# Program order on every engine, and state sums in two steps, in a fused retention and feed-forward kernel

## The chip, the cores and the metric

The kernel runs on one core of one Trainium2 chip. The metric is the time of one execution on the device in microseconds (us); lower is better. The kernel before takes 358.58 us, the median of 3 runs (357.47 to 360.11).

Engines are named as the profile names them: PE is TensorE (matrix products), PEld its weight loads, DVE is VectorE, ACT is ScalarE, POOL is GpSimd, SP is the engine that issues most transfers. PEclk is the clock granted to TensorE, as a share of full speed.

## The reference, cut to what matters

The reference is a retention layer (attention with a decaying causal mask and no softmax), then a feed-forward network (FFN) with an ELU between its two products.

```python
# q, k, v: (8 batches, 8 heads, 576 positions, 64), float32
scores = scale * np.matmul(q, k.transpose(0, 1, 3, 2))
Dmat   = np.where(rel >= 0, gamma ** rel, 0.0)         # rel = query - key position, one gamma per head
x      = np.matmul(scores * Dmat, v)                   # then reordered to (4608 tokens, 512)
h      = x @ w_in                                      # 512 -> 2048
g      = np.where(h > 0, h, np.exp(np.minimum(h, 0)) - 1)
out    = g @ w_out                                     # 2048 -> 512
```

Two facts carry the argument. The decay is a power, so it can be moved into factors on `q` and `k`. What earlier positions contribute can then be kept as a running sum of `k^T v`, the state. And nearly all arithmetic lies in the FFN, so the time on TensorE is set there once the FFN is fed.

## The kernel before

**Units.** A batch is cut into five units. Four of them hold 256 positions of four heads, in the order (first half, heads 0 to 3), (first half, heads 4 to 7), (second half, heads 0 to 3), (second half, heads 4 to 7). The fifth, the tail, holds the last 64 positions of all heads. Units are counted through: 0 to 4 are batch 0, 5 to 9 are batch 1. A unit passes through these steps:

- `load`: three transfers from memory (`rqk`, `rv`).
- `cast`: factors on `q` and `k`, written as bf16 (`qkn`), and a cast of `v` (`vn`). Mostly GpSimd.
- `turn_pe` or `turn`: transpose to `qkT`, on TensorE or by a transposing transfer.
- `scores`, `masks`: products inside chunks of 128 positions, and the causal mask.
- `state`, `prefix`: the state after the first chunk (`mid`) and after the second (`end`). VectorE adds, and GpSimd spreads each to a block-diagonal bf16 tile (`s_mid`, `s_end`).
- `inter`, `values`, `put_x`: products with the states and with `v`, then copies into the FFN input `xt`.

TensorE needs `s_mid` for the second chunk of the same unit. The last engine to touch it is GpSimd, which also does most casts of later units.

**Groups.** The FFN works on nine groups of 512 tokens. Group 0 needs units 0 to 3. Group 1 is done in two pieces: 320 columns (tail of batch 0, first half of batch 1: units 4 to 6) and 192 columns (units 7 and 8). Group 2 needs units of batches 1 and 2, and so on.

**Order of instructions.** `pin` marks an instruction as keeping its written place on its engine. TensorE's products, the loads and the transposing transfers are always pinned. All else goes through `soft`, which pins only until a flag falls. From there the framework's scheduler places those instructions, and it may put them ahead of pinned ones that were written earlier.

```python
pin = tc.keep_in_program_order
early = [True]
def soft(ins):
    return pin(ins) if early[0] else ins

def prefix(u, eng=nc.gpsimd):
    ...                                       # st[0], st[1]: the two chunk sums in PSUM
    if T == 0:
        soft(nc.vector.tensor_copy(mid, st[0]))
    else:
        soft(nc.vector.tensor_tensor(mid, st[0], total[w], ALU.add))
    soft(nc.vector.tensor_tensor(end, st[1], mid, ALU.add))
    total[w] = end
    for dst, src in ((s_mid[w], mid), (s_end[w][T], end)):
        soft(eng.tensor_tensor(dst..., src..., diag..., ALU.mult))

def ffn1(g, ft, lo=0, n=TG, relu=False, nf=1):
    ...                                       # four products into ph for each 128 of the 2048 columns
    soft(nc.scalar.activation(e[:, :m], ph[:, :m], AF.Exp))
    if relu:
        soft(nc.scalar.activation(ph[:, :m], ph[:, :m], AF.Relu))
    else:
        soft(nc.vector.tensor_scalar_add(em[:, :m], e[:, :m], -1.0))
    ...                                       # g from ph and e (relu) or em, on VectorE
```

The program has a start (batch 0, nothing else to do on TensorE), a middle (group 0 of the FFN with units 4 to 6 between its pieces), and a rest in which `step()` handles one unit between FFN pieces. `FT` is 4.

```python
for u in range(FT):                           # the start
    scores(u)
    cast_v(u, "s")
    if u + 1 < FT:
        turn_pe(u + 1, "ss")
    new_x()
    if u:
        inter(u - 1)
        values(u - 1)
    state(u)
    warm(2)                                   # filler products
    if u + 1 < FT:
        masks(u)
        prefix(u)
    ...
    if u + 2 < FT:
        cast(u + 2, "v", None)
last_of_start(FT - 1)
...                                           # FFN of group 0; load(FT) stands before the w_out pieces
cast(FT)                                      # the middle
cast(FT + 1, "v", "s")
...
turn_pe(FT)
stretch(FT)
...
cast(FT + 2, "v", "s")                        # unit 6, before the sums of unit 5
...
turn_pe(FT + 1)
stretch(FT + 1)                               # contains prefix(5)
...
turn_pe(FT + 2)
stretch(FT + 2)                               # contains prefix(6)
finish(FT + 2)
early[0] = False                              # from here the order is free
cast(FT + 3)
...
for ft in range(NFT):
    ffn1(1, ft, 0, 320, relu=ft % 2 == 1)     # first piece of group 1
    if ft == 6:
        turn_pe(FT + 3); stretch(FT + 3)
        cast(FT + 4); cast(FT + 5)            # unit 9 is the tail of batch 1
        load(FT + 8)
    ...
def step():
    stretch(u); load(u + 5); cast(u + 3); turn(u + 2)
```

## Time and profile before

The profiled run of the kernel before took 355.82 us (span 354.1 us). A stage is said to start where ScalarE begins the first exponential of its FFN tiles.

| stage | starts at (us) | TensorE busy in it |
|---|---|---|
| group 0 | 27.3 | |
| group 1, 320 columns | 73.3 | |
| group 1, 192 columns | 94.6 | |
| group 2 | 118.9 | |
| groups 3 to 8 | 149.5 | 99% |
| end of span | 354.1 | |

First the page's table of 40 equal slices, kernel before. One slice is 8.85 us. A digit is the busy share in tenths, or the granted clock in tenths.

```profile
PE   3869988187767997899999999999999999999995
...
POOL 5674889914779779234663687287521220100000
PEclk9987999679899998999999999999999999999999
```

From the eighteenth slice on TensorE is at 9. In the first third there are holes (the 1 in the eighth slice, from 62 us) and clock digits of 6 to 8. GpSimd stands at 9 in that slice. The clock digits of the first two slices mean nothing: the clock's record begins at 20.66 us in this trace.

Second, the busy time by stretch, kernel before, from the end of group 0's first outputs. The next three stretches begin with TensorE's first product of a stage, the last one with the stage itself. Columns: the stretch, its length, then for each engine busy us and instructions, then the mean clock, the DMA share, and GB/s.

```profile
core 0: us, PE busy (x) PEld busy (x) DVE busy (x) ACT busy (x) POOL busy (x), PEclk, DMA share, GB/s
49.90:71.60 21.70, 11.30 (x170) 6.45 (x171) 6.72 (x12) 4.73 (x10) 19.62 (x34) 0.85 1.13 266
71.60:92.70 21.10, 15.54 (x189) 9.65 (x186) 14.24 (x32) 12.00 (x31) 8.67 (x16) 0.90 0.73 159
92.70:117.90 25.20, 18.60 (x327) 12.77 (x330) 13.67 (x32) 9.99 (x25) 20.27 (x35) 0.94 1.07 185
117.90:149.50 31.60, 27.70 (x321) 14.33 (x325) 28.34 (x39) 18.71 (x39) 20.23 (x34) 0.95 0.93 199
149.50:335.00 185.50, 183.99 (x1648) 89.78 (x1670) 125.38 (x196) 105.93 (x207) 73.15 (x124) 1.00 0.42 102
```

In the first stretch TensorE works 11.3 of 21.7 us while GpSimd works 19.6. In the last, which is over half of the span, TensorE works 184.0 of 185.5 us at full clock. A change of order can win nothing there.

Third, the timeline of the first stretch, kernel before: start, duration, engine, line, what was written from what. A bracket gives the idle time before an instruction and what ended it.

```profile
60.37 0.28 DVE L363 COPY mid<-x 128x128 f32<-128x128 f32 x1
60.94 0.60 POOL L212 CAST vn<-rv 128x512 bf16<-128x512 f32 x1
61.51 1.17 POOL L199 TENSOR_TENSOR qkt<-rqt,gq 128x256 bf16<-128x256 f32 x2
62.64 0.60 POOL L200 CAST vt<-rvt 64x512 bf16<-64x512 f32 x1
63.21 0.60 POOL L369 TENSOR_TENSOR s_mid_149<-mid,diag 128x256 bf16<-128x256 f32 x1
63.87 0.28 PE L72 MATMUL x<-qkT,s_mid_149 128*128 128x128 bf16 x2 [2.17 <-POOL s_mid_149 L369]
...
65.69 0.28 DVE L363 COPY mid<-x 128x128 f32<-128x128 f32 x1
66.08 1.19 POOL L187 TENSOR_TENSOR qkn<-rqk,gk 128x256 bf16<-128x256 f32 x2
67.20 0.61 POOL L212 CAST vn<-rv 128x512 bf16<-128x512 f32 x1
67.77 1.17 POOL L187 TENSOR_TENSOR qkn<-rqk,gq 128x256 bf16<-128x256 f32 x2
68.92 1.17 POOL L187 TENSOR_TENSOR qkn<-rqk,gk 128x256 bf16<-128x256 f32 x2
70.06 0.60 POOL L369 TENSOR_TENSOR s_mid_150<-mid,diag 128x256 bf16<-128x256 f32 x1
70.71 0.40 PE L72 MATMUL x<-qkT,s_mid_150 128*128 128x128 bf16 x2 [5.87 <-POOL s_mid_150 L369]
```

`mid` of unit 5 was ready at 60.65 us (60.37 + 0.28), but GpSimd first did a `v` cast, then `qkt` and `vt`. Those two are the tail of batch 1, unit 9, which the program writes only beside the seventh tile of group 1. TensorE waited 2.17 us. For unit 6, seven cast instructions (four lines) came between `mid` and `s_mid`, and TensorE waited 5.87 us.

Last, the one instruction that took longest for its kind, from the timeline of group 2, kernel before:

```profile
135.22 6.28 DVE L446 TENSOR_SCALAR em<-e 128x512 bf16<-128x512 f32 x1 [0.36 <-ACT e L442]
```

The same instruction has a median of 0.43 us. Meanwhile GpSimd ran instructions of 0.6 us back to back. This is called a lockout below. The word is a name for an `em` that takes over 1 us beside such a run; that GpSimd is the cause is not shown.

### The profile page before, as it was taken

The page shows a single profiled execution, that of the slowest core. Times are in us where ns is not written, and L with a number is a line of the kernel's source. Part 1 is how long each engine was busy: PE and PEld are TensorE (multiplying, and loading weights), DVE is VectorE, ACT ScalarE, POOL GpSimd, SP SyncE. Part 2 cuts the span into 40 slices and gives each one's busy share as a digit, 9 for nine tenths or more (in the row PEclk, how much of TensorE's full clock was granted, in tenths as well). Part 3 has the DMA queues.
Part 4 walks back from the last instruction along what each step waited for, and adds up shares of the span by engine and source line. Part 5 has one row for each costly group of instructions (what it writes and reads, how often), then busy time and mean ns, then how long its engine had stood idle before and what let it go on. Part 6 is the DMA issues. An engine that isn't in the chain of part 4 may idle for free.

```text
span 354.1 us, 7848 instructions
## 1 busy us (share of the span) xinstructions
PE 310.5 (88%) x3040; PEld 157.0 (44%) x3084; DVE 219.8 (62%) x379; ACT 180.5 (51%) x366; POOL 177.2 (50%) x313
## 2 busy tenths in 40 slices
PE   3869988187767997899999999999999999999995
PEld 1333444045444553344444544544545454444342
DVE  4646845157566699868676876698666665545500
ACT  3446643155343674555555565555656566555611
POOL 5674889914779779234663687287521220100000
PEclk9987999679899998999999999999999999999999
DMA  8959999991899996663469997953320000110021
GB/s 221 325 165 231 387 302 280 234 267 29 219 177 200 253 184 174 179 182 46 101 167 185 210 176 157 236 142 92 79 58 31 31 31 30 49 42 30 31 81 69
DMA packets 100293, 53.86 MB, mean 152 GB/s; under 512 B 44448, under 2 KB 93600, under 8 KB 100256
## 3 DMA queue, kind: packets, MB, share of 16 engines
q1 hardware_dynamic: 97696, 44.97, 56.3%
q0 software_dynamic: 2560, 8.39, 6.9%
q8 instruction: 24, 0.39, 0.5%
q14 instruction: 13, 0.11, 0.1%
HBM read 36.70 MB, written 9.44 MB: 130 GB/s over the span
## 4 chain that ended last, share of the span: by engine, by line
PE 65%; POOL 12%; DMA 9%; issue 5%; DVE 4%; ACT 2%; SPq 2%; POOLq 0%; ACTq 0%; DVEq 0%
PE pm L72 29%; PE ph L72 28%; POOL qkn L187 6%; PE x L72 5%; DMA rqk<-in_k_dram 3%; DVE em L446 3%; PE sc L72 3%; DMA rvt<-in_v_dram 2%; DMA rv<-in_v_dram 2%; DMA wst<-in_moe_w_out_dram 1%; POOL w_in_sb L147 1%; POOL vn L212 1%; SPq L176 1%; POOL s_mid_149 L369 1%; POOL s_mid_150 L369 1%
## 5 line engine op out<-in xcount | busy, mean ns | idle before, releaser
L72 PE MATMUL ph<-xt,w_in_sb 128*128 128x512 bf16 (+2 forms) x612 | 150.9, 369 | 5.3 <-DVE g L453 2.2
L72 PE MATMUL pm<-w_out_sb,g 128*128 128x512 bf16 x564 | 143.6, 380 | 3.4 <-ACT ot L463 2.1
L442 ACT ACTIVATE e<-ph 128x512 f32<-128x512 f32 (+2 forms) x152 | 87.3, 574 | 94.4 <-PE ph L72 82.1
L72 PEld LDWEIGHTS <-w_in_sb 128*128 128x128 bf16 x640 | 60.9, 100 | 68.4 <-issue 11.1
L72 PEld LDWEIGHTS <-g 128*128 128x128 bf16 x576 | 56.0, 98 | 71.7 <-issue 9.1
L451 DVE SCALAR_TENSOR_TENSOR g<-e,ph 128x512 bf16<-128x512 f32 (+2 forms) x80 | 50.2, 632 | 45.0 <-ACT ph L444 44.7
L446 DVE TENSOR_SCALAR em<-e 128x512 bf16<-128x512 f32 (+2 forms) x76 | 53.0, 697 | 36.3 <-ACT e L442 35.8
L466 POOL DMA_DIRECT2D out_dram<-ot x32 | 18.2, 570 | 88.9 <-ACT ot L463 88.9
L453 DVE SCALAR_TENSOR_TENSOR g<-ph,em 128x512 bf16<-128x512 f32 (+2 forms) x80 | 50.6, 637 | 3.5 <-DVE em L446 0.5
L338 ACT CAST xt<-x 128x256 bf16<-128x256 f32 (+1 forms) x71 | 24.2, 417 | 39.9 <-PE x L72 38.3
L444 ACT ACTIVATE ph<-ph 128x512 f32<-128x512 f32 (+2 forms) x76 | 43.3, 570 | 0.0
L285 DVE TENSOR_TENSOR pt<-sc,mask 128x1024 bf16<-128x1024 f32 x31 | 37.7, 1218 | 8.9 <-PE sc L72 8.9
L187 POOL TENSOR_TENSOR qkn<-rqk,gk 128x256 bf16<-128x256 f32 x64 | 39.9, 641 | 3.3 <-DMA rqk<-in_k_dram 3.2
L187 POOL TENSOR_TENSOR qkn<-rqk,gq 128x256 bf16<-128x256 f32 x52 | 31.1, 617 | 14.9 <-PE x L72 13.6
L463 ACT COPY ot<-pm 128x512 f32<-128x512 f32 x36 | 21.1, 589 | 18.4 <-PE pm L72 18.3
L212 POOL CAST vn<-rv 128x512 bf16<-128x512 f32 x26 | 16.3, 626 | 22.8 <-PE x L72 22.8
L72 PE MATMUL sc<-qkT 64*64 64x128 bf16 (+1 forms) x576 | 17.0, 232 | 3.9 <-ACT qkT L235 2.4
L234 PE MATMUL ptr<-ident,qkn 128*128 128x128 bf16 x64 | 9.0, 260 | 7.4 <-POOL diag L135 4.2
L72 PE MATMUL x<-pt,vn 64*64 64x128 bf16 x504 | 14.3, 232 | 1.1 <-DVE pt L381 1.1
L72 PEld LDWEIGHTS <-qkT 64*64 64x64 bf16 x576 | 10.5, 113 | 9.9 <-ACT qkT L235 3.1
L369 POOL TENSOR_TENSOR s_mid_149<-mid,diag 128x256 bf16<-128x256 f32 x16 | 10.0, 622 | 8.4 <-DVE mid L365 6.3
L369 POOL TENSOR_TENSOR s_mid_150<-mid,diag 128x256 bf16<-128x256 f32 x15 | 9.1, 607 | 9.7 <-DVE mid L363 6.5
(77 smaller groups left out, 181.8 us busy)
## 6 DMA issues: line engine op xcount, KB each, us to landing
rqk<-in_q_dram SPq DMA_DIRECT2D x32, 256.0 KB, 5.2
rqk<-in_k_dram SPq DMA_DIRECT2D x32, 256.0 KB, 4.7
rv<-in_v_dram SPq DMA_DIRECT2D x32, 256.0 KB, 5.4
out_dram<-ot POOLq DMA_DIRECT2D x32, 256.0 KB, 3.1
wst<-in_moe_w_in_dram SPq DMA_DIRECT2D x16, 256.0 KB, 5.3
wst<-in_moe_w_out_dram SPq DMA_DIRECT2D x16, 256.0 KB, 4.9
rqt<-in_q_dram SPq DMA_DIRECT2D x8, 128.0 KB, 4.8
rqt<-in_k_dram SPq DMA_DIRECT2D x8, 128.0 KB, 4.0
```

The lines of the kernel that those rows point to most:

```text
L72: pin(nc.tensor.matmul(*a, **kw))
L187: soft(eng.tensor_tensor(natt[u][0][:, i, e], x[:, e], g[:, e], ALU.mult))
L212: soft(engines[eng](natt[u][1], rawt[u][1]))
L285: soft(nc.vector.tensor_tensor(pt.rearrange("p i h n -> p (i h) n"), sc.rearrange("p i (h n) -> p (i h) n", h=2), mask.rearrange("p k e r ...
L338: soft(engines[eng[c]](dst, src[:, :, :, a // 2 : (a + n) // 2]))
L369: soft(eng.tensor_tensor(dst.rearrange("p h (j d) -> p h j d", j=2), src.unsqueeze(2).to_broadcast([P, 2, 2, D]), diag.unsqueeze(1).unsque ...
L442: soft(nc.scalar.activation(e[:, :m], ph[:, :m], AF.Exp))
L444: soft(nc.scalar.activation(ph[:, :m], ph[:, :m], AF.Relu))
L446: soft(nc.vector.tensor_scalar_add(em[:, :m], e[:, :m], -1.0))
L451: soft(nc.vector.scalar_tensor_tensor(dst, e[:, c], -1.0, ph[:, c], ALU.add, ALU.min))
L453: soft(nc.vector.scalar_tensor_tensor(dst, ph[:, c], 0.0, em[:, c], ALU.max, ALU.min))
L463: soft(nc.scalar.copy(ot, pm))
```

## The change

The intent: every engine runs what the program says in the order in which it is written, so that no cast of a later unit stands before a sum that TensorE waits for. For that the casts have to be written where their loads have landed. In the first batch the state sums are split into two steps, `mid` and `end`, with the masks, transposes and copies of the unit placed around them, and the state products move to just after the scores. The arithmetic stays the same, but for four filler products of 512 columns in the last unit of the start. Two casts change their engine: the `v` cast of unit 5 goes from ScalarE to GpSimd, and half of the `k` cast of unit 3 from GpSimd to VectorE.

```diff
-    early = [True]
-    def soft(ins):
-        return pin(ins) if early[0] else ins
 ...                                  # every soft(...) becomes pin(...)
-    def cast_q(u, eng, i=0):
+    def cast_q(u, eng, i=0, es=(0, 1)):
 ...
+    def prefix_mid(u, eng=nc.gpsimd):
+        ...                          # mid, then s_mid
+    def prefix_end(u, parts=(0, 1)):
+        ...                          # part 0: end; part 1: s_end
 ...
     def last_of_start(u):
 ...
             if hl == 0:
-                prefix(u, nc.vector)
-            else:
-                new_x()
+                prefix_mid(u, nc.vector)
             values(u, (hl,), both[hl])
             inter(u, (hl,), both[hl])
             put_x(u, (hl,), both[hl], ("ss", "sv")[hl])
+            warm(2, ...)                                  # fillers
 ...
     for u in range(FT):
         scores(u)
         cast_v(u, "s")
+        new_x()
+        state(u)
         if u + 1 < FT:
+            masks(u)
             turn_pe(u + 1, "ss")
-        new_x()
+        if u == 0:
+            cast(2, "v", None)
+        if u == 1:
+            cast(3, None, None)
+            cast_q(3, nc.vector)
         if u:
             inter(u - 1)
             values(u - 1)
-        state(u)
-        warm(2)
-        if u + 1 < FT:
-            masks(u)
-            prefix(u)
-        if u:
             put_x(u - 1)
             drop(u - 1)
-        if u + 2 < FT:
-            cast(u + 2, "v", None)
+        if u + 1 < FT:
+            prefix_mid(u)
+        if u == 1:
+            cast_q(3, nc.gpsimd, 1, (0,))
+            cast_q(3, nc.vector, 1, (1,))
+        if u + 1 < FT:
+            prefix_end(u)
+        warm(2)
     last_of_start(FT - 1)
+    prefix_end(FT - 1, (0,))
     for i in range(6):
         w_in_piece(i, "p")
+    prefix_end(FT - 1, (1,))
 ...
     for ft in range(8):
-        if ft == 0:
-            load(FT)
         ...                          # w_out pieces, FFN of group 0
-    for u in range(FT + 1, FT + 6):
+    for u in range(FT, FT + 6):
         load(u)
-    cast(FT)
-    cast(FT + 1, "v", "s")
 ...
-    for part in Q[:2]:
-        ffn2(0, 2, part)
+    cast(FT)
+    ffn2(0, 2, Q[0])
+    ffn2(0, 2, Q[1])
+    cast(FT + 1, "v", "p")
+    ffn2(0, 2, Q[2])
+    ffn2(0, 2, Q[3])
     turn_pe(FT)
     stretch(FT)
-    for part in Q[2:]:
-        ffn2(0, 2, part)
-    cast(FT + 2, "v", "s")
     ffn2(0, 3, Q[0])
     ffn2(0, 3, Q[1])
     turn_pe(FT + 1)
     stretch(FT + 1)
+    cast(FT + 2, "v", "s")
 ...
     finish(FT + 2)
-    early[0] = False
     cast(FT + 3)
```

So the change has three parts: the **order** (the flag is gone), the **start** (split sums and what moves around them), and the **middle** (where the load of unit 4 and the casts of units 4 to 6 stand).

More of the change, by code (lines that the diff above doesn't have):

```diff
@@ L146, in w_in_piece @@
         pin(nc.sync.dma_start(t, moe_w_in[j * P : (j + 1) * P, n * 512 : (n + 1) * 512]))
-        soft(engines[eng](w_in_sb[:, j, n * 512 : (n + 1) * 512], t))
+        pin(engines[eng](w_in_sb[:, j, n * 512 : (n + 1) * 512], t))
     def w_out_piece(f, eng):
@@ L151, in w_out_piece @@
         pin(nc.sync.dma_start(t, moe_w_out[f * P : (f + 1) * P, :]))
-        soft(engines[eng](w_out_sb[:, f, :], t))
+        pin(engines[eng](w_out_sb[:, f, :], t))
     rawt, natt, trt, ptt, score_ps, total = {}, {}, {}, {}, {}, {}
@@ L185, in cast_q @@
         g = (gq, gk)[i][:, 2 * T : 2 * T + 2, 4 * w : 4 * w + 4].unsqueeze(3).to_broadcast([P, 2, 4, D])
-        for e in range(2):
-            soft(eng.tensor_tensor(natt[u][0][:, i, e], x[:, e], g[:, e], ALU.mult))
+        for e in es:
+            pin(eng.tensor_tensor(natt[u][0][:, i, e], x[:, e], g[:, e], ALU.mult))
     def cast(u, q="p", v="p"):
@@ L198, in cast @@
             for hs in (slice(0, H // 2), slice(H // 2, H)):
-                soft(nc.gpsimd.tensor_tensor(qkn[:, hs], rqk[:, hs], g[:, hs], ALU.mult))
-            soft(nc.gpsimd.tensor_copy(vn, rv))
+                pin(nc.gpsimd.tensor_tensor(qkn[:, hs], rqk[:, hs], g[:, hs], ALU.mult))
+            pin(nc.gpsimd.tensor_copy(vn, rv))
         else:
@@ L204, in cast @@
             natt[u] = qkn, vn
-            cast_q(u, nc.vector if q == "v" else nc.gpsimd)
-            cast_q(u, nc.gpsimd, 1)
+            if q:
+                cast_q(u, nc.vector if q == "v" else nc.gpsimd)
+                cast_q(u, nc.gpsimd, 1)
             if v:
@@ L211, in cast_v @@
     def cast_v(u, eng):
-        soft(engines[eng](natt[u][1], rawt[u][1]))
+        pin(engines[eng](natt[u][1], rawt[u][1]))
     def turn_tile(u):
@@ L234, in turn_pe @@
                     pin(nc.tensor.transpose(p[:, j], flat(u)[:, lo : lo + P], ident))
-                soft(engines[eng[i]](trt[u][:, i * 4 : i * 4 + 4], p))
+                pin(engines[eng[i]](trt[u][:, i * 4 : i * 4 + 4], p))
     def queries(u, rows, hl, c):
@@ L278, in masks @@
             pt = ppool.tile([ST, 2, HP, ST], BF16, name="ptt", tag="ptt")
-            soft(nc.vector.tensor_tensor(
+            pin(nc.vector.tensor_tensor(
                 pt, sc[:ST, :, : HP * ST].rearrange("p i (h n) -> p i h n", h=HP),
@@ L284, in masks @@
             pt = ppool.tile([P, 2, 2, 2 * P], BF16, name="pt", tag="pt")
-            soft(nc.vector.tensor_tensor(
+            pin(nc.vector.tensor_tensor(
                 pt.rearrange("p i h n -> p (i h) n"), sc.rearrange("p i (h n) -> p (i h) n", h=2),
@@ L326, in put_x @@
             g, off = divmod(b * S + FT * P, TG)
-            soft(nc.scalar.copy(xt_tile(g)[:, :, off : off + ST], xps[0][:, : HP * ST].rearrange("p (h n) -> p h n", h=HP)))
+            pin(nc.scalar.copy(xt_tile(g)[:, :, off : off + ST], xps[0][:, : HP * ST].rearrange("p (h n) -> p h n", h=HP)))
             return
@@ L337, in put_x @@
                 dst = xt_tile(g)[:, 2 * w + h0 : 2 * w + h1, off : off + n].rearrange("p h (r e) -> p h e r", e=2)
-                soft(engines[eng[c]](dst, src[:, :, :, a // 2 : (a + n) // 2]))
+                pin(engines[eng[c]](dst, src[:, :, :, a // 2 : (a + n) // 2]))
                 a += n
@@ L355, in state, with state_ps, block_diag, prefix @@
                         acc_x(c, i, xps[c][i * D : (i + 1) * D, o : o + D], qkn[cs, 1, e, 2 * hl + i], vn[cs, 2 * hl + i, e])
-    def prefix(u, eng=nc.gpsimd):
-        b, T, w, tail = unit(u)
-        st = [x[:, 2 * P : 3 * P].rearrange("p (h d) -> p h d", h=2) for x in xps]
+    mids = {}
+    def state_ps(c):
+        return xps[c][:, 2 * P : 3 * P].rearrange("p (h d) -> p h d", h=2)
+    def block_diag(dst, src, eng):
+        pin(eng.tensor_tensor(
+            dst.rearrange("p h (j d) -> p h j d", j=2), src.unsqueeze(2).to_broadcast([P, 2, 2, D]),
+            diag.unsqueeze(1).unsqueeze(3).to_broadcast([P, 2, 2, D]), ALU.mult,
+        ))
+    def prefix_mid(u, eng=nc.gpsimd):
+        b, T, w, tail = unit(u)
+        mid = rpool.tile([P, 2, D], FP32, name="mid", tag="mid")
+        if T == 0:
+            pin(nc.vector.tensor_copy(mid, state_ps(0)))
+        else:
+            pin(nc.vector.tensor_tensor(mid, state_ps(0), total[w], ALU.add))
+        mids[u] = mid
+        block_diag(s_mid[w], mid, eng)
+    def prefix_end(u, parts=(0, 1)):
+        b, T, w, tail = unit(u)
+        if 0 in parts:
+            total[w] = rpool.tile([P, 2, D], FP32, name="end", tag="end")
+            pin(nc.vector.tensor_tensor(total[w], state_ps(1), mids.pop(u), ALU.add))
+        if 1 in parts:
+            block_diag(s_end[w][T], total[w], nc.gpsimd)
+    def prefix(u):
+        b, T, w, tail = unit(u)
         mid = rpool.tile([P, 2, D], FP32, name="mid", tag="mid")
@@ L362, in prefix @@
         if T == 0:
-            soft(nc.vector.tensor_copy(mid, st[0]))
+            pin(nc.vector.tensor_copy(mid, state_ps(0)))
         else:
-            soft(nc.vector.tensor_tensor(mid, st[0], total[w], ALU.add))
-        soft(nc.vector.tensor_tensor(end, st[1], mid, ALU.add))
+            pin(nc.vector.tensor_tensor(mid, state_ps(0), total[w], ALU.add))
+        pin(nc.vector.tensor_tensor(end, state_ps(1), mid, ALU.add))
         total[w] = end
-        for dst, src in ((s_mid[w], mid), (s_end[w][T], end)):
-            soft(eng.tensor_tensor(
-                dst.rearrange("p h (j d) -> p h j d", j=2), src.unsqueeze(2).to_broadcast([P, 2, 2, D]),
-                diag.unsqueeze(1).unsqueeze(3).to_broadcast([P, 2, 2, D]), ALU.mult,
-            ))
+        block_diag(s_mid[w], mid, nc.gpsimd)
+        block_diag(s_end[w][T], end, nc.gpsimd)
     def last_of_start(u):
@@ L378, in last_of_start @@
         ptt[u] = pt
-        both = [[ps_h.tile([P, 512], FP32, name="o2", tag="ph") for _ in range(2)], None]
+        both = [[ps_h.tile([P, 512], FP32, name="o2", tag="ph") for _ in range(2)],
+                [ps_m.tile([P, 512], FP32, name="o3", tag="pm"), ps_h.tile([P, 512], FP32, name="o3", tag="ph")]]
         for hl in range(2):
-            soft(nc.vector.tensor_tensor(
+            pin(nc.vector.tensor_tensor(
                 pt[:, :, hl], sc.rearrange("p i (h n) -> p i h n", h=2)[:, :, hl],
@@ L391, in last_of_start @@
             put_x(u, (hl,), both[hl], ("ss", "sv")[hl])
+            warm(2, both[1][1] if hl == 0 else ps_s.tile([P, 2, 512], FP32, name="warm", tag="sc")[:, 0])
         drop(u)
@@ L441, in ffn1 @@
         m = n * nf
-        soft(nc.scalar.activation(e[:, :m], ph[:, :m], AF.Exp))
+        pin(nc.scalar.activation(e[:, :m], ph[:, :m], AF.Exp))
         if relu:
-            soft(nc.scalar.activation(ph[:, :m], ph[:, :m], AF.Relu))
+            pin(nc.scalar.activation(ph[:, :m], ph[:, :m], AF.Relu))
         else:
-            soft(nc.vector.tensor_scalar_add(em[:, :m], e[:, :m], -1.0))
+            pin(nc.vector.tensor_scalar_add(em[:, :m], e[:, :m], -1.0))
         for f in range(nf):
@@ L450, in ffn1 @@
             if relu:
-                soft(nc.vector.scalar_tensor_tensor(dst, e[:, c], -1.0, ph[:, c], ALU.add, ALU.min))
+                pin(nc.vector.scalar_tensor_tensor(dst, e[:, c], -1.0, ph[:, c], ALU.add, ALU.min))
             else:
-                soft(nc.vector.scalar_tensor_tensor(dst, ph[:, c], 0.0, em[:, c], ALU.max, ALU.min))
+                pin(nc.vector.scalar_tensor_tensor(dst, ph[:, c], 0.0, em[:, c], ALU.max, ALU.min))
     def ffn2(g, it, fts, pool=None, tag="pm"):
@@ L462, in ffn2, with warm @@
             ot = opool.tile([P, DM], FP32, name="ot", tag="ot")
-            soft(nc.scalar.copy(ot, pm))
+            pin(nc.scalar.copy(ot, pm))
             i0 = g * TG + it * P
             store = nc.sync if g == NTG - 1 else nc.gpsimd
-            soft(store.dma_start(out[i0 : i0 + P, :], ot))
-    def warm(n):
-        if n:
-            d = ps_h.tile([P, TG], FP32, name="warm", tag="ph")
-            for _ in range(n):
-                mm(d, ident, zero, start=True, stop=True)
+            pin(store.dma_start(out[i0 : i0 + P, :], ot))
+    def warm(n, d=None):
+        d = ps_h.tile([P, TG], FP32, name="warm", tag="ph") if d is None else d
+        for _ in range(n):
+            mm(d, ident, zero, start=True, stop=True)
     def last_unit(g):
```

## The prediction

> **What bounds the kernel now.** There are two regimes. In the busy-time table by stretch, TensorE is busy 187.6 of 189.2 us from 145.8 to 335 us at a granted clock of 1.00: nothing but TensorE work matters there. The first 145.8 us are different. TensorE is busy 12.0 of 22.6 us (49.9 to 72.5), 14.8 of 20.2 (72.5 to 92.7), 18.6 of 25.2 (92.7 to 117.9) and 24.1 of 27.9 (117.9 to 145.8), and the clock is 0.50 from 25.3 to 30.9 us. There the chain of waits runs through GpSimd casts and loads. From 50 to 120 us it gives GpSimd `qkn` 24%.
>
> **What costs the time.** In the timeline, casts of later units stand ahead of the state sums on GpSimd. `mid` was written at 60.4 us and its `s_mid` only began at 63.2; TensorE sat idle 2.17 us. The next one cost 5.87 us (`mid` 65.7, `s_mid` 70.1), and the clock then stayed halved until about 76 us. Similar waits of 0.9 to 2.1 us follow at 92, 102, 106, 111 and 115 us. At 135.2 us a VectorE `em`, 0.43 us at its median, took 6.28 us beside an unbroken GpSimd run. [...]
>
> **What the change moves.** No arithmetic to speak of is added: about four more filler matmuls (0.22 us each at full clock).
> 1. Start. The split sums and earlier state matmuls take the k-cast to transpose to sum loop (4.54 us per unit now) apart. Following my estimate in the new order with traced durations, FFN work starts near 23.8 us instead of 25.3, and fillers probably keep the clock up (now 5.6 us at 0.50 lose 2.8 us). The weight casts begin earlier, so the load queue's gap at 18.8 to 22.5 us (19 to 45 GB/s) closes. Gain about 4 us by 50 us.
> 2. 50 to 72.5 us. In program order `s_mid` follows `mid` at once: both waits shrink to the 1.5 to 2 us of mask, copy and product. Casting unit 6 (the third of the second batch) after the sums costs about 2 us back. Second-group FFN starts near 64 us; cumulative gain 8 us.
> 3. 72.5 to 120 us. GpSimd loses its hoisted lead, but its idle time (8.3 us before 80.7, 4.2 before 88.4, 4.1 before 98.8) shrinks. This stretch stays bound by GpSimd, about 4.2 us per unit (five casts of 0.6, two sums of 0.6). Cumulative gain 10 to 13 us.
> 4. After that TensorE bounds; no gain. The 6.28 us lockout may go, or come back elsewhere, as GpSimd runs become longer.
>
> Shrinking the sum somewhat for lockouts and cold clocks, I expect 346 us, range 338 to 353: faster by over 2% 0.80, within 2% 0.17, slower 0.03.
>
> **What would show each step.** First `ph` matmul near 24 us with 0.22 us per 512 columns, not 0.43; waits of TensorE on `s_mid` under 2 us around 55 to 65 us; first 320-column `ph` matmul near 64 us; GpSimd near full from there to 105 us; 99% busy TensorE afterwards, its stretch unshortened.
>
> **What would make it wrong.** A TensorE still at half clock in the start [...]; `em` starved beside the longer GpSimd runs, directly on the path while 320-column FFN tiles take 0.65 us each; transposing loads waiting for late casts between 85 and 95 us; in-order queues adding waits in the steady part, where free order was already at 99%.

The sum came to 10 to 13 us. That fillers keep the clock up is the author's expectation. The clock of that trace was at half from 65.0 to 75.3 us, a little less long than stated. One slip in it: unit 6 is the third of units 4, 5 and 6, but the second unit of the second batch. Unit 4 is the tail of the first.

## The result, and the profile after

| | median (us) | runs | range |
|---|---|---|---|
| before | 359.28 | 4 | 357.47 to 360.11 |
| after | 339.89 | 4 | 339.27 to 341.77 |

The ratio is 0.9476, with a 95% interval of 0.942 to 0.9531: faster. A ratio in this document is the mean time of one kernel's fast runs over that of the other's fast runs of the same rounds, so it is not quite the ratio of the medians that are quoted. The prediction's class was right, and its range of 338 to 353 us holds the result. Its centre of 346 us was 6 us too high.

The profiled run of the changed kernel took 339.58 us, a typical one, while that of before was a fast one. The two traces differ by 16.2 us in span, the medians by 19.4 us. The traces therefore explain 16.2 us.

| stage | before starts at | after starts at | gain so far (us) |
|---|---|---|---|
| group 0 | 27.3 | 23.2 | 4.1 |
| group 1, 320 columns | 73.3 | 65.3 | 8.0 |
| group 1, 192 columns | 94.6 | 84.1 | 10.5 |
| group 2 | 118.9 | 108.3 | 10.6 |
| groups 3 to 8 | 149.5 | 133.8 | 15.8 |
| last exponential | 334.6 | 318.3 | 16.2 |
| end of span | 354.1 | 337.9 | 16.2 |

The page's slices, kernel after (8.45 us each):

```profile
PE   3877997777769999999999999999999999999995
...
POOL 5586955528989799243585568566665120000100
PEclk9999999599899999999999999999999999999999
```

The hole of 1 in TensorE's row is gone. One clock digit of 5 is left, at about 60 us.

The busy time by stretch, kernel after; columns and stages as before:

```profile
46.10:63.60 17.50, 12.24 (x170) 6.86 (x171) 7.41 (x14) 4.82 (x10) 9.97 (x17) 0.88 1.12 292
63.60:82.60 19.00, 15.04 (x189) 9.50 (x186) 13.84 (x31) 11.91 (x31) 9.79 (x17) 0.93 0.30 77
82.60:107.30 24.70, 18.65 (x327) 13.07 (x330) 14.86 (x34) 10.06 (x26) 23.74 (x42) 0.93 1.11 233
107.30:133.80 26.50, 26.14 (x321) 13.58 (x325) 23.01 (x39) 18.76 (x40) 23.03 (x39) 1.00 1.26 222
133.80:318.70 184.90, 183.57 (x1648) 89.73 (x1670) 119.14 (x196) 105.81 (x207) 81.03 (x135) 1.00 0.49 117
```

The first stretch shrinks from 21.7 to 17.5 us, and GpSimd's work in it from 34 instructions to 17: the casts of later units have left it. They come back in the third stretch (35 instructions before, 42 after) and in the last (124 and 135). The fourth stretch, group 2, shrinks by 5.1 us: TensorE is now busy 99% of it at full clock. The last is the same within 0.6 us.

The timeline of the two sums, kernel after:

```profile
55.73 0.28 DVE L387 COPY mid<-x 128x128 f32<-128x128 f32 x1
56.16 0.60 POOL L359 TENSOR_TENSOR s_mid_149<-mid,diag 128x256 bf16<-128x256 f32 x1 [4.17 <-DVE mid L387]
...
61.70 0.28 DVE L387 COPY mid<-x 128x128 f32<-128x128 f32 x1
62.07 0.60 POOL L359 TENSOR_TENSOR s_mid_150<-mid,diag 128x256 bf16<-128x256 f32 x1 [2.69 <-DVE mid L387]
...
62.73 0.40 PE L67 MATMUL x<-qkT,s_mid_150 128*128 128x128 bf16 x2 [1.58 <-POOL s_mid_150 L359]
```

Now GpSimd waits for `mid` (4.17 and 2.69 us idle) and starts the sum at once. The product with `s_mid` of unit 5 has no wait listed, that of unit 6 has 1.58 us in place of 5.87.

The longest waits of TensorE between 48 and 146 us (what waited, what for; us in total, times, longest). First before, then after:

```profile
PE x L72 <- POOL s_mid_150 L369: 10.5, 4, 5.9
PE x L72 <- POOL s_mid_149 L369: 6.8, 4, 2.2
```

```profile
PE x L67 <- POOL s_mid_150 L359: 2.7, 2, 1.6
PE sc L67 <- DMA qkT<-qkn: 2.5, 2, 2.0
...
PE x L67 <- POOL s_mid_149 L359: 0.8, 1, 0.8
```

Waits for `s_mid` fall from 17.3 to 3.5 us. A wait for transposing transfers (`qkT<-qkn`) is new.

### The profile page after: what moved, and what is told of

Same layout as the page of the kernel before. It is cut to its first block, busy times and chain, and to the rows that moved or that the text cites. A ratio compares the mean times of both kernels' runs of the same rounds, so it can differ in the third digit from the quotient of the medians.

```text
span 337.9 us, 7844 instructions
## 1 busy us (share of the span) xinstructions
PE 305.2 (90%) x3044; PEld 156.5 (46%) x3088; DVE 207.5 (61%) x379; ACT 179.3 (53%) x365; POOL 179.3 (53%) x314
## 4 chain that ended last, share of the span: by engine, by line
PE 73%; DVE 9%; DMA 6%; POOL 4%; ACT 4%; issue 2%; SPq 1%; DVEq 0%; ACTq 0%; POOLq 0%
PE pm L67 34%; PE ph L67 30%; PE x L67 4%; PE sc L67 3%; DVE pt L281 2%; DMA wst<-in_moe_w_in_dram 2%; DMA rqk<-in_q_dram 2%; DVE g L472 2%; DMA qkT<-qkt 1%; DVE em L467 1%; DMA qkT<-qkn 1%; DVE g L474 1%; POOL qkn L182 1%; SPq L171 1%; ACT xt L334 1%
## 5 line engine op out<-in xcount | busy, mean ns | idle before, releaser
L67 PE MATMUL ph<-xt,w_in_sb 128*128 128x512 bf16 (+2 forms) x611 | 147.3, 361 | 4.6 <-DVE g L474 1.3
L67 PEld LDWEIGHTS <-w_in_sb 128*128 128x128 bf16 x640 | 60.0, 99 | 65.6 <-issue 6.8
L467 DVE TENSOR_SCALAR em<-e 128x512 bf16<-128x512 f32 (+2 forms) x76 | 42.1, 554 | 32.2 <-ACT e L463 32.1
L182 POOL TENSOR_TENSOR qkn<-rqk,gk 128x256 bf16<-128x256 f32 x63 | 37.9, 621 | 4.2 <-DMA rqk<-in_k_dram 4.2
L359 POOL TENSOR_TENSOR s_mid_150<-mid,diag 128x256 bf16<-128x256 f32 x15 | 9.2, 615 | 26.1 <-DVE mid L387 12.6
L208 POOL CAST vn<-rv 128x512 bf16<-128x512 f32 x27 | 17.9, 663 | 0.0
L67 PEld LDWEIGHTS <-qkT 64*64 64x64 bf16 x576 | 10.5, 112 | 13.3 <-ACT qkT L231 5.1
L230 PE MATMUL ptr<-ident,qkn 128*128 128x128 bf16 x64 | 8.0, 252 | 7.4 <-DVE qkn L182 5.2
L67 PE MATMUL x<-pt,vn 64*64 64x128 bf16 x496 | 13.6, 226 | 0.0
```

The source lines that it names most:

```text
L67: pin(nc.tensor.matmul(*a, **kw))
L182: pin(eng.tensor_tensor(natt[u][0][:, i, e], x[:, e], g[:, e], ALU.mult))
L359: pin(eng.tensor_tensor(dst.rearrange("p h (j d) -> p h j d", j=2), src.unsqueeze(2).to_broadcast([P, 2, 2, D]), diag.unsqueeze(1).unsquee ...
L467: pin(nc.vector.tensor_scalar_add(em[:, :m], e[:, :m], -1.0))
```

## The experiments

**The theory and its rivals.** Theory A (order): the free order lets casts of later units in ahead of the sums; most of the gain is the order alone, and the start alone is worth 4 us at most. Rival B (placement): the new start and middle bring the gain themselves, whatever the order. Rival C (lockout): the main gain is that the long `em` (2.7 to 6.3 us in the kernel before) are gone. Twelve kernels were run, each beside runs of the kernel before. Medians are compared within a call; across calls, ratios.

### The order alone: p_only

```diff
 # from before
     finish(FT + 2)
-    early[0] = False
     cast(FT + 3)
```

> The kernel before with one line taken out, so that VectorE, ScalarE and GpSimd keep program order to the end; start and middle as before. Theory (order): the main gain comes from the state sums no longer standing behind casts of later units on GpSimd, so this alone gives about 10 us (349 us, ratio 0.97), the TensorE waits on s_mid of 2.2 and 5.9 us at 60 to 71 us fall under 2 us each, and first 320-column ph starts near 66 us. Rival (start): the gain comes from the new start and its clock, and this alone gives under 3 us.

Measured: 344.42 us against 358.59 us, ratio 0.9603 (0.9571 to 0.9635), faster. One deleted line brings 14.2 us, more than theory A expected. TensorE's waits between 48 and 146 us, kernel p_only:

```profile
PE sc L72 <- DMA qkT<-qkn: 4.8, 4, 2.2
PE x L72 <- POOL s_mid L369: 3.2, 3, 1.9
```

The waits for `s_mid` have fallen to 3.2 us with the old start and the old middle. Over the twelve sums that follow the start, the time between the end of `mid` and the beginning of `s_mid` adds up to 20.3 us in the kernel before and to 2.5 us here.

One thing was not tested. The deleted line pins VectorE, ScalarE, GpSimd and the stores at once, and no run pins GpSimd alone. That the order on GpSimd is what counts rests on these waits, and not on a run of its own.

### The start alone: start_only

```diff
 # from before: the new start, with the old middle; soft() and its flag stay
+    def prefix_mid(...)  /  prefix_end(...)  /  new loop over the first units
```

> The new start (loop, split sums, fillers) with the middle as before and free order after the second batch began. Theory (order): 3 to 4 us earlier at 50 us, but GpSimd casts still stand ahead of the sums afterwards, so at most 4 us in the end (355 us, ratio 0.99). Rival (start): 9 us or more (350 us or less).

Measured: 355.66 us against 358.59 us, ratio 0.9934 (0.9865 to 1.0003), the same within 2%. About 3 us by the medians, and by the interval hardly told from nothing. That is as theory A had it; rival B falls for the start.

### The middle alone: mid_only

```diff
 # from before: the new middle, with the old start; soft() and its flag stay
-        if ft == 0:
-            load(FT)
-    cast(FT)
-    cast(FT + 1, "v", "s")
+    ...                                  # placed as in the change
```

> Only the placement of loads and casts of units 4 to 6 as in the change; old start, free order later. Theory (order): within 2 us of the kernel before, because later casts are still hoisted ahead of the sums; rival (placement): the casts' placement is what matters, 5 us or more.

Measured: 359.19 us against 358.59 us, ratio 1.002 (0.9976 to 1.0063), the same. Placing the casts by itself is worth nothing.

### Start and middle without the order: start_mid

```diff
 # from after
+    early = [True]
+    def soft(ins):
+        return pin(ins) if early[0] else ins
 ...                                      # pin(...) back to soft(...) but for TensorE and the transfers
     finish(FT + 2)
+    early[0] = False
     cast(FT + 3)
```

> The changed kernel with free order restored from the second group on (the flag back at its old place). Theory (order): gives back 10 us or more of the 19 (350 us or more), and TensorE waits on s_mid at 55 to 70 us come back. Rival (start and placement): stays within 4 us of the changed kernel (344 us or less).

Measured: 357.15 us against 358.59 us, ratio 0.9968 (0.993 to 1.0006), the same. Everything but the order is there, and the gain is 1.4 us. Kernel start_mid, waits of TensorE from 48 to 152 us:

```profile
PE x L72 <- POOL s_mid L364: 14.3, 7, 6.8
```

The waits for `s_mid` are back (14.3 us; 17.3 before). The four runs settle the main question: without the order the rest is worth about nothing, and the order alone brings 14.2 us. Theory A stands, and rival B falls. The profiles of all kernels of this document agree: between 48 and 146 us TensorE waits 14.3 to 17.3 us for `s_mid` in the five with free order, and 2.4 to 4.8 us in the nine with program order.

### The order with only one of the other parts: start_pin and mid_pin

```diff
 # start_pin, from after: the old middle
+        if ft == 0:
+            load(FT)
+    cast(FT)
+    cast(FT + 1, "v", "s")
 ...
 # mid_pin, from after: the old start (loop over the first units and last_of_start as in before)
```

> New start and program order to the end, but loads and casts of units 4 to 6 placed as before. If the effects of order (14 us alone) and start add up, 341 us; the placement in the middle is then worth about 1 us. If the placement is needed for the start's 4 us to survive, 344 us.

> Program order to the end and the new placement in the middle, with the old start. If placement is worth nothing by itself: 344 us, as with order alone. If it is the start that adds the last 4 us, then the changed kernel (339.9 us) is 4 us faster than this one.

Measured, against 357.05 us: start_pin 341.88 us, ratio 0.9567 (0.9511 to 0.9623); mid_pin 343.65 us, ratio 0.9634 (0.9582 to 0.9685). Order and middle together are no better than order alone (p_only, 0.9603), in ratio. Order and start together are a little better than order alone, but the intervals overlap. The stage starts of the profiles say more:

| stage starts (us) | p_only | mid_pin | start_pin | after |
|---|---|---|---|---|
| group 0 | 25.8 | 28.1 | 23.5 | 23.2 |
| group 1, 320 columns | 68.5 | 68.8 | 68.8 | 65.3 |
| group 2 | 113.3 | 114.6 | 113.4 | 108.3 |
| groups 3 to 8 | 138.5 | 139.8 | 138.6 | 133.8 |

With the old start group 0 begins anywhere from 25.8 to 28.3 us in the profiles (27.3 in the kernel before), with the new one from 23.1 to 25.1 us, so single differences of 1 us here mean nothing. But start_pin begins early, at 23.5 us, and has lost all of it by 68.8 us. Its timeline shows one place where: the first product that needs a cast piece of `w_out`, first in start_pin, then in after:

```profile
35.85 1.01 PE L67 MATMUL pm<-w_out_sb,g 128*128 128x512 bf16 x2 [4.47 <-POOL w_out_sb L147]
```

```profile
32.93 0.59 PE L67 MATMUL pm<-w_out_sb,g 128*128 128x512 bf16 x2 [1.47 <-POOL w_out_sb L147]
```

In start_pin TensorE waits 4.47 us here, and its mean clock is 0.69 from 30 to 40 us. In after the wait is 1.47 us and the clock 1.00. This suggested that the early start makes TensorE reach the `w_out` pieces before they have landed, and that moving the load of unit 4 behind them repairs it. The run load_early below tests that. A caution: the profiled runs of start_pin (344.44 us) and of mid_pin (345.64 us) were the slowest of their four.

### Are the fillers needed: no_fill

```diff
 # from after
     put_x(u, (hl,), both[hl], ("ss", "sv")[hl])
-            warm(2, both[1][1] if hl == 0 else ps_s.tile(...)[:, 0])
```

> The changed kernel without the four filler matmuls between the halves of the last start unit. Theory (clock): the first FFN tiles run at 0.43 us per 512 columns again for some us, so that eight tiles end about 2.5 us later; but TensorE waits 1.5 us for the first w_out cast at 33 us anyway, so only 1 to 1.5 us is left in the end (341 us). Rival: the clock holds without them, no change in the width of the matmuls and 340 us.

Measured in 5 rounds: 340.13 us against 357.05 us, ratio 0.9526 (0.9488 to 0.9565), span 337.7 us where after has 337.9 us. The mean clock was 1.00 up to 46 us and 0.88 from 46 to 64 us; after has 1.00 and 0.87. The first FFN products start as early and run as fast; first after, then no_fill:

```profile
22.12 2.75 PE L67 MATMUL ph<-xt,w_in_sb 128*128 128x512 bf16 x12
```

```profile
22.00 2.76 PE L67 MATMUL ph<-xt,w_in_sb 128*128 128x512 bf16 x12
```

That is 0.23 us a product (2.75 / 12) with or without them. The prediction had the clock kept up "probably" by fillers. In this profile it stays up without the four new ones: from 18.9 to 22.3 us TensorE was busy 1.99 of 3.4 us, where after, with them, was busy 2.36 of 3.4 us from 18.5 to 21.9 us, and the clock of both was at 1.00 to 46 us. The eight fillers that the kernel before has too stayed in. The clock's record begins at 15.1 us in after and at 20.7 us in before; the last filler product of 512 columns ahead of it took 0.63 and 0.61 us, the first one behind it 0.39 and 0.38 us. That the new start's denser work brings the clock up earlier and keeps it up is not shown by a run of its own.

### Casts one place earlier: shift

After the order is fixed, GpSimd stands idle for 7.56 us before the sum of unit 7, while casts that could be done are written later. This run writes the casts of units 8 to 11 and the transposes one place earlier.

```diff
 # from after
     cast(FT + 3)
+    cast(FT + 4)
 ...
         if ft == 6:
-            cast(FT + 4); cast(FT + 5)
+            cast(FT + 5); cast(FT + 6); turn(FT + 5)
         if ft == 13:
-            cast(FT + 6); turn(FT + 5)
+            turn(FT + 6); cast(FT + 7)
     finish(FT + 4)
-    turn(FT + 6); cast(FT + 7)
```

> The changed kernel with the casts of units 8 to 11 (and the DMA transposes of 9 and 10) moved one place earlier, into GpSimd's idle time at 51 to 74 us. Theory (GpSimd bounds 74 to 105 us): the idle stretch of 7.6 us before 73.6 shrinks to about 4.6, and the work after it ends 2 to 3 us earlier (337 us). Rival (TensorE and VectorE bound that stretch): no change (340 us).

Measured: 339.09 us against 357.05 us, ratio 0.9484 (0.9434 to 0.9534); beside no_fill 1.0 us less, with intervals that overlap. The sum of unit 7, first in after, then in shift:

```profile
73.64 0.61 POOL L359 TENSOR_TENSOR s_mid_149<-mid,diag 128x256 bf16<-128x256 f32 x1 [7.56 <-DVE mid L389]
```

```profile
72.63 0.61 POOL L359 TENSOR_TENSOR s_mid<-mid,diag 128x256 bf16<-128x256 f32 x1 [5.32 <-DVE mid L389]
```

GpSimd's idle time fell by 2.2 us and the waits for `s_mid` from 3.5 to 2.4 us. But TensorE's waits changed to this, kernel shift, 48 to 146 us:

```profile
PE sc L67 <- DMA qkT<-qkn: 4.8, 3, 2.6
PE x L67 <- POOL s_mid L359: 2.4, 3, 1.9
```

The waits for transposing transfers (`qkT<-qkn`) stand at 4.8 us, where after has 2.5 us. It is not shown that this run's edit raised them: in the other seven kernels with program order and this order of issue they lie between 2.5 and 6.7 us, with 6.7 us in no_fill. But they are the longest on this list.

### The transposes ahead of the loads: turn_first

In `step()` the transposing transfer stands behind the three loads of a later unit on the same issuing engine. These loads are of 256 KB (128 KB for a tail), and in shift TensorE waits 4.8 us for transposes. The author's guess was that a transpose waits for the loads issued ahead of it. Then exchanging the two should remove the wait.

```diff
 # from shift
     def step():
         stretch(u)
-        load(u + 5)
         cast(u + 3)
         turn(u + 2)
+        load(u + 5)
```

> The kernel with casts one place earlier (339.1 us) and, in each step, the DMA transposes issued before the loads of a later unit instead of after them. Theory: with GpSimd's backlog gone, TensorE waits for transposes that queue behind three 256 KB loads (4.8 us in that trace); those waits fall to under 2 us, 335 to 337 us. Rival (the DMA engines are simply full there): the waits move to the casts, no change.

Measured: 335.5 us (335.2 to 336.46) against 358.80 us, ratio 0.9363 (0.9306 to 0.942), within what was expected. It beats both kernels. The list of TensorE's waits from 48 to 146 us has no line for `qkT<-qkn` any more, where the eight other kernels with program order have 2.5 to 6.7 us. The longest wait is now this, twice what it was in shift; kernel turn_first:

```profile
PE x L67 <- POOL s_mid L359: 4.8, 4, 1.9
```

The run shows that the order of issue decides these waits: 4.8 us in shift, none listed here. By what mechanism is not shown: between 80 and 110 us these transposes still take 5.1 us at the median from issue to landing (4.2 us in after), and how much of the gain is a shorter queue and how much the earlier issue is not separated. Busy time from 81 to 107 us, first turn_first, then after:

```profile
81.00:107.00 26.00, 22.14 (x405) 15.03 (x410) 18.05 (x42) 13.64 (x32) 25.26 (x43) 1.00 1.14 234
```

```profile
81.00:107.00 26.00, 19.93 (x348) 13.95 (x353) 16.00 (x37) 10.87 (x27) 24.70 (x43) 0.93 1.06 222
```

TensorE gets 22.1 us of work done in place of 19.9, at full clock, with GpSimd busy 25.3 of 26.0 us. That stretch is still bound by GpSimd.

### What the lockouts are worth: before_noem and after_noem

In the kernel before, five `em` took over 1 us: 6.28, 2.72, 2.72, 2.72 and 2.83 us. In after the longest took 0.88 us. The other free-order kernels look alike: in each of start_only, mid_only and start_mid one `em` took 5.9 to 8.2 us. In p_only, with program order, the longest took 0.89 us. Rival C holds that this is the main gain. Both runs replace `em` on VectorE by the variant with a Relu on ScalarE in groups 2 to 8, one in before and one in after as the control of what the edit itself costs.

```diff
 # in f1(g), of before and of after
-        return [lambda ft=ft: ffn1(g, ft, relu=ft % 2 == 1) for ft in range(NFT)]
+        return [lambda ft=ft: ffn1(g, ft, relu=True) for ft in range(NFT)]
```

> The kernel before, with every 512-column FFN tile of groups 2 to 8 in the form that has no em (ScalarE does the relu, VectorE one product less; same values). [...] Theory (order): the long lockouts (6 us once, 2.7 us four times in the free-order kernels, none in the ordered ones) lie mostly beside the critical path; VectorE's longest instruction falls to 1.2 us, but only 1 to 3 us of time go (356 us). Rival (lockout): the lockouts are what program order removed, so 8 us or more go here (350 us or less).

> The same edit on the changed kernel, as a control for what the edit costs by itself. There are no long lockouts to remove: within 2 us of the changed kernel (340 us) under both theories; what it differs by is the edit's own price on ScalarE.

Measured, against 358.80 us: before_noem 356.11 us, ratio 0.9897 (0.9807 to 0.9987); after_noem 342.48 us, ratio 0.9553 (0.9476 to 0.9631). So before gains about 1% without its lockouts. The control loses 0.8% against after's own ratio (0.9553 against 0.9476), though their intervals overlap. They were run at other times. In the profiles group 2 takes 30.6 us in before, 29.1 in before_noem, 25.4 in after and 27.3 in after_noem. If the edit costs before the 1.9 us that it costs after (27.3 − 25.4), taking the lockout away in group 2 is worth up to 3.4 us (30.6 − 29.1 + 1.9); without that assumption, 1.5 us. That is a part of the 5.2 us that group 2 gained, and not the main gain. (Each of these times is from one profile, and the profiled runs of the noem pair were the slowest of their four.) Rival C falls as the main cause and stays as a minority share.

The order is no guarantee against a lockout. In after_noem, which is in program order, an `em` of group 1 took 4.79 us, from its timeline:

```profile
106.64 4.79 DVE L467 TENSOR_SCALAR em<-e 128x384 bf16<-128x384 f32 x1 [2.11 <-ACT e L463]
```

Part of what after_noem lost may be this. What sets the long ones apart was looked for in the traces. In the kernel before 46 `em` began inside a GpSimd instruction: 41 of them met at most two such instructions, the five long ones five to eleven. The same phase is found with both outcomes: about 0.34 us into a GpSimd instruction one `em` took 2.83 us (before, at 242.65 us) and another 0.55 us (after, at 109.0 us). It stays open.

### The load of unit 4 ahead of the w_out loads: load_early

```diff
 # from after
     for ft in range(8):
+        if ft == 0:
+            load(FT)
 ...
-    for u in range(FT, FT + 6):
+    for u in range(FT + 1, FT + 6):
         load(u)
```

> The changed kernel with the load of unit 4 back in its old place, ahead of the w_out loads on the queue; nothing else moved. Theory: this is what ate the start's gain where the middle stayed as before: TensorE's wait for the first w_out cast grows from 1.5 to about 4 us, the clock may drop after it, and the kernel takes 342 us. Rival (the casts' places did it): no change, 340 us.

Measured: 340.97, 341.76, 350.14 and 346.42 us against 358.80 us. The last two were slow (clock 0.969 and 0.975; 0.985 in the profiled run) and are not used. The two fast ones give a ratio of 0.9522 (0.9434 to 0.961); after has 0.9476, so 0.0046 or some 1.6 us less. The wait for the first `w_out` piece, kernel load_early:

```profile
33.52 0.59 PE L67 MATMUL pm<-w_out_sb,g 128*128 128x512 bf16 x2 [1.89 <-POOL w_out_sb L147]
```

It grew from 1.47 to 1.89 us only, not to the 4.47 us of start_pin. The expected size of the wait was missed. The 1.6 us rest on two runs and lie inside the intervals, so neither the expectation nor its rival (no change) is shown. Comparing the instruction streams says more: up to this product load_early and start_pin are the same program. So the 4.47 us of start_pin can't be put down to its code alone. Between 22.5 and 26 us its transfers moved 231 GB/s, those of load_early 286, and its pieces landed later. Why they were slower in that execution is open; the rate alone does not say it, since after moved 212 GB/s there, with no load of unit 4 ahead of the pieces, and waited least. What start_pin's profile had lost by 68.8 us was therefore in part a spread between executions, and its own median (341.88 us) is the better measure.

How the last 4 us beyond the order divide between start and middle stays open. The nearest comparison is this: mid_pin 343.65, start_pin 341.88 and no_fill, which has both parts, 340.13 us.

## Why the prediction was right, and where its sizes were off

**Point 1, the start: right in size, in part by luck.** It expected 4 us and the traces show 4.1. The first FFN product came at 22.12 us, earlier than the 23.8 predicted (25.33 before): 3.2 us were won there, where 1.5 were forecast, and less was left for the clock. The gap of the load queue closed: from 18.8 to 22.5 us 112 GB/s moved, where before had 30. The products ran at full clock, and in no_fill they did so without the four new fillers.

What the prediction called "a TensorE still at half clock in the start" as a danger did not come in this profile. In the kernel before, the clock was at 1.00 from 20.7 to 24.1 us, with TensorE busy 1.87 of these 3.4 us, and then at 0.50 to 30.9 us. In after TensorE was busy 2.36 of the 3.4 us from 18.5 to 21.9 us, just ahead of its first FFN product, and the clock held. What decides whether it falls is not shown.

But the same start can end otherwise. The kernels start_only and start_mid run the same instructions on TensorE as after up to the first FFN product. Their mean clock over the first 25 us was 0.93, where after has 1.00. Group 0 began at 24.7 and 25.1 us there, 1.5 and 1.9 us later than in after. So a part of the 4.1 us is likely luck.

**Point 2, the middle: right.** Predicted cumulative gain 8 us by the start of the second group, measured 8.0. Both waits for `s_mid` fell under 2 us (none, and 1.58). Casting unit 6 after the sums was to cost about 2 us; the small waits of TensorE on `qkn` from 57.11 to 58.90 us sum to 1.43 us (0.50 + 0.47 + 0.18 + 0.28), and a half-clock stretch from 59.4 to 66.3 us follows (from 56.0 to 59.4 us TensorE was busy 1.86 of 3.4 us, with no listed wait over 0.50 us). The first 320-column product came at 63.62 us, as predicted (64).

**Point 3, 72.5 to 120 us: right at its lower end.** Predicted 10 to 13 us, measured 10.5 at the 192 columns and 10.6 at group 2. GpSimd was not near full from 64 us as stated: it had that idle stretch of 7.56 us before 73.64 us, and filled up from there. In the 26 us from 81 to 107 it was busy 24.70.

**Point 4, "After that TensorE bounds; no gain": the mis-sized term.** It measured 5.2 us in group 2 (30.6 to 25.4 us), and the order brings it: group 2 takes 25.2 to 25.4 us in the eight kernels with program order that keep every `em`, p_only among them, and 30.5 to 33.1 us in the four with free order that keep them. TensorE's busy share there was 27.7 of 31.6 us at a mean clock of 0.95 before, and 26.1 of 26.5 at 1.00 after. The prediction had named the 6.28 us lockout and priced it at nothing ("may go, or come back elsewhere"). It went, and so did the wait of 2.11 us on `s_mid` before 136.7 us and the half-clock stretch behind them (136.7 to 140.1 us). The noem pair puts the lockout's share of these 5.2 us at 1.5 to 3.4 us. In groups 3 to 8 the statement was right: 185.1 and 184.6 us.

**The sum.** Points 1 to 3 gave 10 to 13 us and 10.6 came; point 4 gave none and 5 came. The forecast was also shrunk "somewhat" for risks that did not come, to 346 us. That is 12.6 us below 358.58, where the traces show 16.2 and the medians 19.4. The further 3 us between the two are the spread of the runs of before: its profiled run was a fast one.

**What the experiments add.** The prediction took order, start and middle as one change. In the runs the order alone brings 14.2 us, start and middle without it 1.4 us. On top of it they bring some 4 us (0.9603 less 0.9476 is 0.0127, or 4.6 us of 359).

## What to carry to other kernels

Where an engine both serves the critical path with short instructions and prepares later work, look at the timeline for what stands between an input's arrival and the short instruction; a scheduler that fills idle time may put exactly the wrong work there. Fix the order first and place the work after: here the placement was worth nothing before the order held. When a fixed order has removed one wait, look at the list of waits again, transfers too: here waits for transposes, issued behind loads, came up with the order (2.5 to 6.7 us). Issuing the transposes first took these waits away, and the time fell by another 3 to 4 us (shift to turn_first, across two calls).
